# Projecting the first queries from raw activations and correcting them for layer normalisation afterwards

## The chip, the cores and the metric

The kernel runs on one NeuronCore of a Trainium2 chip. The metric is the device time of one execution in microseconds (us); the time before is 212.38 us, the median of 3 runs.

## The reference

A transformer block of 2048 tokens and width 640, in bfloat16: the input is normalised, and a local dilated attention and a dense GELU network run side by side on the normalised tokens; both results are added to the raw input.

```python
xn  = layernorm(x)                        # (x - mean) / sqrt(var + 1e-5), no affine part
qkv = xn @ wqkv                           # 640 -> 3*640; 32 heads of 20
# each token attends to itself and 7 earlier ones, 2 apart: s, s-2, ..., s-14
logits = einsum(q, k gathered) * 20**-0.5 ; attn = softmax(logits, over the 8)
A = einsum(attn, v gathered) @ wo
B = gelu(xn @ w1 + b1) @ w2 + b2          # 640 -> 1536 -> 640
return x + A + B
```

## The kernel before, in words

The tokens are split into 4 chunks of 512 (`CH`), each of 4 blocks of 128 rows. A chunk goes through these stages:

- **Statistics and normalisation.** VectorE takes mean and variance of each block (`st`, L409 and L411; the block's halves are two instructions); ScalarE takes the square root (`rs`, L430), VectorE the reciprocal (`rc`, L434). In the first chunk (n = 0) VectorE normalises (`xn`, L450), TensorE transposes 128x128 pieces (`tp`, L465), and VectorE or ScalarE copies them into `xnT` (`tc`, L470). In later chunks ScalarE normalises (L446) and a transposing DMA, issued from SyncE, writes `xnT` (L477). Block 1 of the first chunk has its sums taken on ScalarE (`sm`, `sq`, L417 and L426).
- **Projections.** In chunk 0, q of the first two blocks is made in 50 matmuls of 128 columns (`ga`, `gb`, `gd`, `ge`, L522), each as soon as a block's transposes are there; k, v and the second half of q are made in pairs of blocks, 256 columns wide (`hj`, L553). A name such as `hj011` is read which matrix (0 q, 1 k, 2 v), which pair of blocks, which group of output rows. Later chunks use 512 columns (`pj`, L509). ScalarE copies the results from PSUM (`gc`, `hc`, `pc`).
- **Attention.** VectorE multiplies q by the eight shifted k (`qk`, L583, 8 instructions per chunk), TensorE sums over each head (`lg`, L608), VectorE and ScalarE do the softmax, DMAs spread the weights over 128 partitions (`xd`, `xs`), VectorE multiplies v (`av`, L681) and adds (`ad`, `ot`).
- **Dense network.** TensorE makes the hidden layer in 12 pieces a chunk (`f1`, L703; pieces 0 to 5 use the first half of `w1_sb`, 6 to 11 the second), ScalarE applies GELU (`ge`, L714), and TensorE adds the second layer and the output projection in one accumulation (`o`, L734 and L736).

All work of PE, DVE, ACT and SP is issued in one order written out by hand, the list `ORDER`; each engine takes its own tasks from it in that order and waits where an input is late. A planner's costs (`make_plan`) stand in the file but only the list decides. POOL is scheduled by the program text. PSUM has four rotating banks for projections and hidden pieces (`psA`), two for logits (`psL`) and two for outputs (`psO`).

The inputs arrive through one queue issued from SyncE: x block 0, then `wq`, `wk`, x blocks 2 and 3, `wv`, the other x, and the two halves of `w1`; x block 1 and `b1` are issued from ScalarE. Ten matmuls on constants (`WARM`, L776) run while nothing has arrived.

```python
def load_w(s):
    nc.sync.dma_start(wqkv[s][:], wqkv_v[:, :, s * D : (s + 1) * D])
...
for name in ORDER:
    pieces[name]["fn"]()
```

Of the kernel before, what the change touches and what calls it, by code (L numbers as in the profile page):

```python
# [77 lines left out]
WARM = 10  # L78
# [6 lines left out]
pad01 pad02 st00a st00 sm rs00 me nm rc00 sq xn00a xn00b tp00a tp00b tc00a rs01 tb ga tc00b rc01 xn01 gb2 b1 tp01  # L85
gb3 tc01a tc01b gb4 gd gc0 ge st03a hj101 gc4 st03 st02a rs03 hj102 st02 hc101 hj100 rs02 hc102 rc02 rc03 gc1 hj200
xn03 xn02 hc100 st11a tp03 tp02 st13a tc03 hj201 st11 tc02 st10a hj202 hc200 st12a hj012 st10 hj010 st13 hc012 hc202
st12 hj111 hc010 hc201 hj011 rs1 hc111 rc1 st21a hj110 hc011 st22a st22 hj112 hc110 st20a hj212 st33a hc112 f102
xn10 qk031 hc212 f100 xn13 tc10 qk001 ge02 f109 qk020 hj210 pad11 tc13 ge09 hj211 qk010 xn11 f108 hc211 qk000 ge00
f101 tc11 qk011 f105 ge01 ge08 qk021 f104 xn12 f1011 tc12 ge04 qk030 f1010 ge011 st23a st21 lg00 ge010 st20 ld lg01  # L90
ge05 st23 lg02 lg03 st31a rs2 pj114 mk m0 pj102 pc114 st32a st30a pj110 pc102 mx0 hc210 pj111 pc110 st32 ex0 pj101
rc2 st31 st30 pj100 st33 pj112 ss0 pc100 pc101 pj104 xn21 ri0 pj103 tc21 pc104 at0 pc111 pj113 pc103 pc112 pj123
pc113 xn23 qk120 f113 pc123 tc23 xn22 f103 qk111 pj121 ge03 qk121 f118 xd0 qk130 ge13 f107 ge18 f112 qk100 ge07
pad21 f106 ge12 qk110 xs0 f115 ge06 qk131 xw0 f110 rs3 qk101 o020 tc22 xn20 o021 ge15 lg10 lg11 av011 lg12 pc121
tc20 lg13 ge10 rc3 pj120 av000 o022 pc120 av031 xn32 o023 pj122 tc32 av021 f111 pc122 m1 xn30 pj124 ge11 av030 tc30
pad12 pj214 av020 pj204 pc214 pj203 pc204 av001 pj211 pc203 av010 pc124 pj202 xn33 mx1 pc211 pj210 tc33 xn31 ad01
pj221 pc210 pc202 pj223 tc31 pj201 ad00 pj220 pc201 pc223 pj213 xp0 pj200 pc213 ad02 pc221 pj212 pc220 pc200 pj224
pc212 ex1 xb0 ot0 pj310 f1110 qk231 pc310 o024 qk220 pj300 oc02 ss1 pad31 od02 o000 o001 qk200 o002 o003 ri1 o004
at1 pj313 qk201 xd1 oc00 o010 pc313 qk211 pc300 pj301 xs1 qk210 o011 o012 qk221 o013 xw1 pj303 qk230 o014 xp1 xb1
lg20 oc01 lg21 av130 pc303 lg22 pc224 lg23 av100 o030 f138 av110 o031 od00 ge38 av111 pj312 o032 pc301 m2 ge110 f117  # L100
pc312 av131 f116 av120 pj304 pj302 mx2 o033 pc302 av121 ge16 f121 ge17 ad11 f1111 xp2 f1210 ge21 xb2 ge111 o034
ge210 av101 pad22 pc304 f119 ad10 pj311 pj222 pc311 xb3 oc03 pj314 ad12 ge19 od01 f114 od03 f125 ge14 pc222 ot1
pj324 pad32 pc314 ex2 o100 qk331 pj322 qk321 o101 ge25 o102 ss2 o103 pj323 ri2 o104 qk330 pc323 pc322 pj320 at2 oc10
pj321 pc320 qk311 xd2 xs2 o110 pc324 qk301 o111 pc321 o112 qk310 f120 qk300 f126 xw2 f130 ge26 qk320 f127 xl lg30
ge27 lg31 av201 lg32 lg33 o113 m3 o114 av211 f1311 oc11 av200 od11 o120 o121 od10 av221 o122 av230 o123 o124 av220
f1211 oc12 mx3 od12 o130 av210 o131 ge20 ge30 f124 ex3 ad20 f123 o132 ge311 o133 av231 o134 ge24 ss3 f128 ge211 oc13
f129 ad21 ge23 f122 ge29 ge28 f131 ge22 ri3 o210 at3 f135 ad22 o211 xd3 f134 f1310 ot2 o212 ge310 ge31 o213 xs3 o214
xw3 f137 oc21 ge34 od21 o220 av311 o221 o222 av300 o223 av310 o224 f136 av321 oc22 od22 o230 av301 o231 od13 o232
av320 o233 av331 o234 av330 f132 oc23 od23 o200 ad31 o201 ge32 ge36 o202 ge37 f139 ad30 f133 ge39 ge35 o203 ge33
o204 ad32 o310 oc20 o311 o300 ot3 o301 o302 o303 o304 o312 oc30 o313 od30 o320 od20 o321 o322 o323 o314 o324 oc31  # L110
od31 o330 oc32 o331 od32 o332 o333 o334 ohi oclo ochi
# [3 lines left out]
def make_plan(fns, offsets={}):  # L115
# [11 lines left out]
    def turned(n, pair=None):  # L127
        if n:
            return [f"tc{n}{bl}" for bl in range(BPC)]
        every = ["tc00a", "tc00b", "tc01a", "tc01b", "tc02", "tc03"]  # L130
        return every if pair is None else every[4 * pair : 4 + 4 * pair]

    def done(n, which):
        if n:
            return [f"pc{n}{which}{to}" for to in range(KT)]
        return (["gc0", "gc1", "gc4"] if which == 0 else [f"hc{which}0{g}" for g in range(len(COLS))]) + [
            f"hc{which}1{g}" for g in range(len(COLS))
        ]

    pl.add("tb", PE, 0.1, -99, ["tp00b"], f("tb"))  # L140
    pl.add("b1", VE, 0.1, -90, ["tb"], f("b1"))
    for n in range(NCH):
        base = n * PERIOD
        prev = base - PERIOD
        early = base + (-37.0 if n == 1 else -85.0)
        xnT, q, k, v, oT = (("xnT", n), ("q", n), ("k", n), ("v", n), ("oT", n))
        hTs = [("hT", n, ft) for ft in range(FT)]

        for bl in range(BPC):
            land = (3.2, 3.65, 9.3, 9.3)[bl] if n == 0 else (0.0, 13.3, 17.6, 17.6)[n]  # L150
            r = -40 if n else -90
            if n == 0 and bl == 1:
                pl.add("sm", SE, 0.84, -99, [], f("sum1"), after=land)
                pl.add("nm", SE, 0.22, -99, ["sm"], f("neg1"))
                pl.add("me", VE, 0.12, -98, ["sm"], f("mean1"))
                pl.add("sq", SE, 0.93, -99, ["nm"], f("sq1"))
                pl.add("rs01", SE, 0.3, -99, ["sq"], f("sqrt", 0, 1, 2), table="sqrt")
                pl.add("rc01", VE, 0.16, -99, ["rs01", "me"], f("rstd", 0, 1, 2))
                continue
            pl.add(f"st{n}{bl}a", VE, 0.42, r, [], f("st", n, bl, 0), [("stats", n, bl)], land)  # L160
# [4 lines left out]
        if n > 0:  # L165
            pl.add(f"rs{n}", SE, 0.3, -98, [f"st{n}{bl}" for bl in range(BPC)], f("sqrt", n, 0, BPC), table="sqrt")
            pl.add(f"rc{n}", VE, 0.25, early + -4.0, [f"rs{n}"], f("rstd", n, 0, BPC))
        for bl in range(BPC):
            xn, tp = ("xn", n, bl), ("acc", "tp", n, bl)
            if n > 0:  # L170
                pl.add(f"xn{n}{bl}", SE, 0.81, early + -4.0, [f"rc{n}"], f("xn", n, bl), [xn])
                pl.add(f"tc{n}{bl}", DQ, 3.0 if n > 1 else 2.7, early - 3.0, [f"xn{n}{bl}"], f("td", n, bl), [xn, xnT], 23.0)
                continue

            if bl == 0:
                for u, a, b, eng, own in (("a", 0, 2, VE, "lo"), ("b", 2, KT, SE, "hi")):
                    us = (b - a) / KT
                    pl.add(f"xn00{u}", VE, 0.06 + 0.5 * us, -99, ["rc00"], f("xn", 0, 0, a, b), [xn])
                    pl.add(f"tp00{u}", PE, 0.54 * us, -99, [f"xn00{u}"], f("tp", 0, 0, a, b, own), [xn])
                    pl.add(f"tc00{u}", eng, 0.16 + 0.49 * us, -99, [f"tp00{u}"], f("tc", 0, 0, a, b, eng), [xnT])  # L180
                continue
            pl.add(f"xn0{bl}", VE, 0.42, -99, [f"rc0{bl}"], f("xn", 0, bl), [xn])
            pl.add(f"tp0{bl}", PE, 0.3, -99, [f"xn0{bl}"], f("tp", 0, bl, 0, KT), [xn, tp])
            for u, a, b, eng in (("a", 0, 2, VE), ("b", 2, KT, SE)) if bl == 1 else (("", 0, KT, SE),):
                pl.add(f"tc0{bl}{u}", eng, 0.16 + 0.49 * (b - a) / KT, -100 if bl == 1 else -99, [f"tp0{bl}"], f("tc", 0, bl, a, b, eng), [tp, xnT])
# [10 lines left out]
        if n == 0:  # L196
            wq, wk, wv = 6.1, 8.5, 11.6
            A, B, C = ("acc", "qa"), ("acc", "qb"), ("acc", "qc")
            pl.add("ga", PE, 0.056 * 10, -60, ["tc00a"], f("ga", 0, 2), [xnT, A, B], wq)
            pl.add("gb2", PE, 0.056 * 5, -60, ["tc00b", "ga"], f("ga", 2, 3), [xnT, A, B], wq)  # L200
            pl.add("gb3", PE, 0.056 * 5, -60, ["gb2"], f("ga", 3, 4), [xnT, A, B], wq)
            pl.add("gb4", PE, 0.056 * 5, -60, ["gb3"], f("ga", 4, KT), [xnT, A, B], wq)
            pl.add("gd", PE, 0.056 * 10, -59, ["tc01a", "gb4"], f("gd", 0, 2), [xnT, B, C], wq)
            pl.add("ge", PE, 0.056 * 15, -59, ["tc01b", "gd"], f("gd", 2, KT), [xnT, B, C], wq)
            pl.add("gc0", SE, 0.54, -50, ["gb4"], f("gc", 0), [A, q])
            pl.add("gc1", SE, 0.54, -50, ["ge"], f("gc", 1), [C, q])
            pl.add("gc4", SE, 0.3, -50, ["ge"], f("gc", 4), [B, q])
            for which, buf, land in ((0, q, wq), (1, k, wk), (2, v, wv)):
                for pair in range(0 if which else 1, 2):
                    for g, (a, b) in enumerate(COLS):  # L210
                        ps = ("acc", "gp", which, pair, g)
                        nm = pl.add(f"hj{which}{pair}{g}", PE, 0.55 * (b - a), -50 + which // 2, turned(0, pair), f("gp", which, pair, a, b), [xnT, ps], land)
                        pl.add(f"hc{which}{pair}{g}", SE, 0.3 * (b - a), -50, [nm], f("gq", which, pair, a, b), [ps, buf])
        for which, buf in enumerate((q, k, v)):
            for to in range(KT if n else 0):
                ps = ("acc", "p", n, which, to)
                r = early + (0 if which < 2 else 20.0)
                pl.add(f"pj{n}{which}{to}", PE, 1.08, r, turned(n), f("pj", n, which, to), [xnT, ps])
                pl.add(f"pc{n}{which}{to}", SE, 0.52, early + 0.0, [f"pj{n}{which}{to}"], f("pc", n, which, to), [ps, buf])
            if which:  # L220
                need = done(n - 1, which) if n else []
                bufs = [buf] + ([("k" if which == 1 else "v", n - 1)] if n else [])
                pl.add(f"pad{n}{which}", SE, 0.26, early if n else -50, need, f("pad", n, which), bufs)
# [64 lines left out]
def kernel(  # L288
# [37 lines left out]
    outp = ctx.enter_context(tc.tile_pool(name="outp", bufs=2))  # L326

# [7 lines left out]
    nc.gpsimd.memset(b1_rt[:], 0.0)  # L335
# [8 lines left out]
    def load_w(s):  # L344
        nc.sync.dma_start(wqkv[s][:], wqkv_v[:, :, s * D : (s + 1) * D])  # L345
# [465 lines left out]
```

## Time and profile before

| | |
|---|---|
| time, median of 3 runs (lowest, highest) | 212.38 us (212.26, 212.46) |
| profiled execution: its own time | 212.62 us |
| its span (first to last instruction) | 210.6 us |
| PE (matmul) busy | 205.5 us, 98% |
| DVE busy | 173.4 us, 82% |
| ACT busy | 111.7 us, 53% |
| POOL busy | 19.8 us, 9% |
| moved by DMA | 23.93 MB, mean 114 GB/s |

The profile is of one execution, which took 212.62 us; 2.0 us of that lie outside the span of its instructions. PE is TensorE's matmul queue, PEld its weight loads, DVE is VectorE, ACT ScalarE, POOL GpSimd, SP SyncE (SPq and POOLq are the DMA-issuing sides of their queues). "x" before a number counts instructions. In a timeline a row is a start, a duration, and the merged instructions; square brackets give the idle time before them and what ended it. A matmul's listed duration includes its passage through the array, so a row of them is shorter than the sum of its parts.

### The profile page before, as it was taken

Reading aid. Unit: us, or ns where it says so; the run is one execution under the profiler, and the core shown is the slowest. Engines: PE = TensorE matmul, PEld = TensorE weight load, DVE = VectorE, ACT = ScalarE, POOL = GpSimd, SP = SyncE. Lnnn points to the kernel's source line nnn. Section 1 sums busy time; section 2 is a strip of 40 time slices with the busy share of each in tenths; the row PEclk is TensorE's granted clock in tenths of the full one; section 3 lists DMA queues with packets and bytes.
Section 4 is the critical chain, followed back from the end, with each engine's and each line's share of the span. In section 5 each row is a group of like instructions: output and inputs, shape, how many; then the busy total and the mean of one; then the engine's idle time right before and its main releaser. Section 6 shows DMA issues by size and latency. Waiting matters only on the chain.

```text
span 210.6 us, 3645 instructions
## 1 busy us (share of the span) xinstructions
PE 205.5 (98%) x1511; PEld 118.5 (56%) x1535; DVE 173.4 (82%) x178; ACT 111.7 (53%) x193; POOL 19.8 (9%) x37
## 2 busy tenths in 40 slices
PE   8999999999999999999999999999999999999994
PEld 2999656554465555555654555565554455555552
DVE  3587998969979999997899999989999829997001
ACT  5576977889786748330727487321396221441120
POOL 2000000000000002110400600101101011101130
PEclk9999999999999999999999999999999999999999
DMA  6999416924932173569296690621122571212224
GB/s 221 364 363 372 90 33 188 382 56 82 142 72 42 20 187 34 93 94 224 79 150 218 93 156 3 139 93 13 24 29 34 100 127 21 24 27 31 31 21 75
DMA packets 24072, 23.93 MB, mean 114 GB/s; under 512 B 9080, under 2 KB 21880, under 8 KB 24056
## 3 DMA queue, kind: packets, MB, share of 16 engines
q1 hardware_dynamic: 17008, 14.68, 25.1%
q0 software_dynamic: 4144, 4.92, 17.5%
q10 hardware_dynamic: 2904, 4.10, 7.0%
q8 instruction: 12, 0.20, 0.4%
q14 instruction: 4, 0.03, 0.1%
HBM read 10.00 MB, written 7.54 MB: 83 GB/s over the span
## 4 chain that ended last, share of the span: by engine, by line
PE 87%; DMA 7%; SPq 4%; issue 1%; DVE 0%
PE lo L734 27%; PE hps L703 24%; PE pps L509 23%; PE hi L736 8%; DMA w_sb<-in_B_w_dram 7%; PE L L608 4%; SPq L342 2%; SPq L359 2%; PE gps L553 1%; SPq L345 1%; DVE osb L764 0%
## 5 line engine op out<-in xcount | busy, mean ns | idle before, releaser
L703 PE MATMUL hps<-xnT,w_sb 128*128 128x512 bf16 x235 | 55.3, 379 | 0.3
L681 DVE TENSOR_TENSOR pv<-vT,ax 128x2560 bf16<-128x2560 bf16 x32 | 45.8, 1483 | 9.1 <-DMA ax<-attn 4.6
L734 PE MATMUL lo<-w_sb,hT 128*128 128x512 bf16 x184 | 52.9, 379 | 0.1
L583 DVE TENSOR_TENSOR prod<-qT,kT 128x2560 bf16<-128x2560 bf16 x32 | 45.5, 1483 | 1.9 <-ACT kT L568 1.5
L714 ACT ACTIVATE hT<-hps,b1T 128x512 bf16<-128x512 f32 x48 | 31.6, 689 | 18.4 <-PE hps L703 16.9
L736 PE MATMUL hi<-w_sb,hT 128*128 128x128 bf16 x192 | 40.3, 219 | 0.5 <-issue 0.2
L703 PEld LDWEIGHTS <-w_sb 128*128 128x128 bf16 x240 | 22.8, 98 | 26.3 <-DMA w_sb<-in_B_w_dram 0.6
L690 DVE TENSOR_TENSOR pv<-pv 128x5120 bf16<-128x5120 bf16 x12 | 33.7, 2821 | 0.2
L741 ACT CAST osb<-lo 128x512 bf16<-128x512 f32 x15 | 8.8, 587 | 44.7 <-issue 26.7
L734 PEld LDWEIGHTS <-hT 128*128 128x128 bf16 x192 | 18.7, 98 | 22.5 <-issue 0.4
L734 PE MATMUL lo<-wo,oT 128*128 128x512 bf16 x74 | 21.9, 379 | 0.0
L747 POOL DMA_DIRECT2D out_dram<-osb x15 | 13.6, 904 | 86.2 <-ACT osb L742 80.1
L736 PEld LDWEIGHTS <-hT 128*128 128x128 bf16 x192 | 18.4, 98 | 2.7
L509 PE MATMUL pps<-xnT,wk_sb 128*128 128x512 bf16 x73 | 18.2, 379 | 0.1
L509 PE MATMUL pps<-xnT,wv_sb 128*128 128x512 bf16 x72 | 18.0, 379 | 0.1
L509 PE MATMUL pps<-xnT,wq_sb 128*128 128x512 bf16 x75 | 18.0, 379 | 0.1
L736 PE MATMUL hi<-wo,oT 128*128 128x128 bf16 x80 | 16.9, 219 | 0.3
L409 DVE BATCH_NORM_STATS2 stats<-x_sb 128x6 f32<-128x320 bf16 x30 | 13.0, 467 | 4.2 <-DMA x_sb<-in_A_x_dram 4.2
L490 POOL DMA_DIRECT2D out_dram<-b2bc x4 | 5.3, 1465 | 98.6 <-DMA out_dram<-x_sb 98.6
L568 ACT CAST qT<-pps 128x512 bf16<-128x512 f32 x15 | 8.7, 590 | 8.8 <-PE pps L509 8.8
L734 PEld LDWEIGHTS <-oT 128*128 128x128 bf16 x80 | 7.8, 98 | 9.4
L509 PEld LDWEIGHTS <-wk_sb 128*128 128x128 bf16 x75 | 8.6, 118 | 7.3 <-issue 0.2
(75 smaller groups left out, 198.7 us busy)
## 6 DMA issues: line engine op xcount, KB each, us to landing
w_sb<-in_B_w_dram SPq DMA_DIRECT2D x4, 960.0 KB, 11.4
out_dram<-osb POOLq DMA_DIRECT2D x15, 160.0 KB, 3.4
ax<-attn SPq DMA_DIRECT2D x8, 256.0 KB, 4.7
ax<-attn ACTq DMA_DIRECT2D x8, 256.0 KB, 4.3
out_dram<-b2bc POOLq DMA_DIRECT2D x3, 640.0 KB, 6.6
x_sb<-in_A_x_dram SPq DMA_DIRECT2D x1, 1280.0 KB, 14.0
out_dram<-x_sb ACTq DMA_DIRECT2D x1, 1120.0 KB, 4.6
wq_sb<-in_A_wqkv_dram SPq DMA_DIRECT2D x1, 800.0 KB, 4.8
```

The source lines that it names most:

```text
L409: nc.vector.bn_stats(stats[:, i, :], x_sb[:, b, i * (D // 2) : (i + 1) * (D // 2)])
L509: nc.tensor.matmul(ps[:], lhsT=wqkv_p[which][:, ti, to, :], rhs=xnT[:, ti, :], start=(ti == 0), stop=(ti == KT - 1),)
L568: nc.scalar.copy(dest[:, to, off : off + CH], tiles["pps", n, which, to][:])
L583: nc.vector.tensor_tensor(out=prod[:, i, :, :], in0=qkv_tile(n, 0)[:], in1=qkv_tile(n, 1)[:, :, off : off + CH], op=ALU.mult,)
L681: nc.vector.tensor_tensor(out=pv[:, i, :, :].rearrange("p t (j c) -> p t j c", j=BPC), in0=qkv_tile(n, 2)[:, :, off : off + CH].rearrange( ...
L690: nc.vector.tensor_tensor(out=ta[:], in0=ta[:], in1=tb[:], op=ALU.add)
L703: nc.tensor.matmul(ps[:], lhsT=w1_sb[:, ti, ft * P : (ft + 1) * P], rhs=tiles["xnT", n][:, ti, :], start=(ti == 0), stop=(ti == KT - 1),)
L714: nc.scalar.activation(hT[:], tiles["hps", n, ft][:], ACT.Gelu_apprx_tanh, bias=b1T[:, ft : ft + 1], scale=1.0)
L734: nc.tensor.matmul(lo[:], lhsT=lhs, rhs=rhs[:, 0:CH], start=first, stop=last)
L736: nc.tensor.matmul(hi[:, 0 : D - CH], lhsT=lhs, rhs=rhs[:, CH:D], start=first, stop=last)
L741: nc.scalar.copy(osb[:, 0:CH], tiles["lo", n, bl][:])
L747: nc.gpsimd.dma_start(rows, tiles["osb", n, bl][:], accum_op=ALU.add)
```

## The change

- **q of blocks 0 and 1 from raw x.** TensorE transposes the raw blocks (`tr`, 10 transposes), VectorE copies them to a tile `xr` (`ra`, `rb`, in two cuts per block) beside columns of ones, and 30 matmuls (`qr0`, `qr1`, `qr2`; 20 of 258 columns and 10 of 130) give the raw projection together with the column sums of `wq`, in the logits' and outputs' PSUM banks. Layer normalisation is affine per token, so q = (raw - mean x column sum) / deviation: the means and reciprocal deviations (`rn`) are written to DRAM (`rw`) and read back spread over 128 partitions (`rr`), both by POOL's DMA queue; VectorE subtracts (`qc0`, `qc1`) and GpSimd multiplies (`qd0`, `qd1`). The 50 matmuls L522 and the copies `gc0`, `gc1`, `gc4` go. Normalisation and transposes of the blocks stay, since k, v and the dense network use them; block 0 is no longer cut in two.
- **wq and wv arrive in two loads each**, cut after row tile 2 of 5; v of the first pair begins with the first part (`hv0`, `hv1`, loops turned so that the row tile is outermost).
- **Statistics of the last chunk on ScalarE**: sums (`su`), negated means (`nq`) and squares (`sv`), and `mq` on VectorE, in place of eight `st` instructions and four aggregations.
- **Smaller ones**: 6 warm-up matmuls, not 10; `b1` loaded by POOL's queue and its transpose `tb` placed after the first k piece; `w2` in one load; `ORDER` written anew throughout, with the same tasks otherwise.

The core of the diff (the new order is cut to its beginning):

```diff
-WARM = 10
+WARM = 6
...
-pad01 pad02 st00a st00 sm rs00 me nm rc00 sq xn00a xn00b tp00a tp00b tc00a rs01 tb ga tc00b rc01 xn01 gb2 b1 tp01
-gb3 tc01a tc01b gb4 gd gc0 ge st03a hj101 gc4 st03 st02a rs03 hj102 st02 hc101 hj100 rs02 hc102 rc02 rc03 gc1 hj200
-xn03 xn02 hc100 st11a tp03 tp02 st13a tc03 hj201 st11 tc02 st10a hj202 hc200 st12a hj012 st10 hj010 st13 hc012 hc202
-st12 hj111 hc010 hc201 hj011 rs1 hc111 rc1 st21a hj110 hc011 st22a st22 hj112 hc110 st20a hj212 st33a hc112 f102
-xn10 qk031 hc212 f100 xn13 tc10 qk001 ge02 f109 qk020 hj210 pad11 tc13 ge09 hj211 qk010 xn11 f108 hc211 qk000 ge00
+st00a tr0 st00 sm tr1 ra0 rs00 ra1 nm rb1 sq qr0 rc00 xn00 rb0 rs01 pad01 me tp00 rc01 pad02 xn01 qr1 tc00 rn tp01
+rw qr2 tc01a tc01b hj101 st02a tb st02 hj100 rr st03a rs02 hc101 b1 hj102 rc02 xn02 hc100 st03 tp02 hj202 hc102 rs03
+hv0 tc02 rc03 xn03 st13a tp03 hv1 st11a tc03 st11 hc202 qc0 hj110 hc201 hj012 st13 hc110 qd0 hj010 st10a hc200 st12a
+hc012 qc1 hj112 hc010 hj111 hc112 st10 qd1 hj011 st12 hc111 st23a rs1 hj212 rc1 hc011 hj211 xn10 qk030 xn11 f102
+qk031 hc211 tc10 hj210 hc212 ge02 qk020 f109 f105 qk021 ge09 tc11 hc210 f1010 pad11 qk000 ge05 f104 xn12 qk010 ge010
...
-    def load_w(s):
-        nc.sync.dma_start(wqkv[s][:], wqkv_v[:, :, s * D : (s + 1) * D])
+    def load_w(s, *cuts):
+        for a, b in zip((0, *cuts), (*cuts, KT)):
+            nc.sync.dma_start(wqkv[s][:, a:b, :], wqkv_v[:, a:b, s * D : (s + 1) * D])
...
-    nc.scalar.dma_start(b1_rt[0:FT, :], B_b1.rearrange("(t p) -> t p", p=P))
-    load_w(0)
+    load_w(0, 2)
     load_w(1)
     load_x(2, BPC)
-    load_w(2)
+    load_w(2, 2)
...
+    nc.gpsimd.dma_start(b1_rt[0:FT, :], B_b1.rearrange("(t p) -> t p", p=P))
...
+    def do_su(bl):
+        nc.scalar.activation(sink[:], x_sb[:, LAST + bl, :], ACT.Identity, accum_out=acc3[:, bl : bl + 1])
+    def do_sv(bl):
+        b = LAST + bl
+        nc.scalar.activation(
+            sink[:], x_sb[:, b, :], ACT.Square, bias=neg3[:, bl : bl + 1], scale=RD, accum_out=mv[:, b, 1:2]
+        )
...
+    def do_qr(a, b):
+        qL, qlo, qhi = q_raw()
         for ti in range(a, b):
+            first, last = ti == 0, ti == KT - 1
+            for to, ps in enumerate((qL[:, 0, 0:WIDE], qL[:, 1, 0:WIDE], qlo[:, 0:WIDE], qhi[:, 0:WIDE])):
+                nc.tensor.matmul(
+                    ps,
+                    lhsT=wqkv_p[0][:, ti, to, :],
+                    rhs=xr[:, ti, ONE : BOTH + 2],
+                    start=first,
+                    stop=last and to > 1,
+                    skip_group_check=True,
+                )
...
+    def do_rw():
+        nc.gpsimd.dma_start(rn_d[:], rn[:])
+    def do_rr():
+        tiles["rnbc"] = axp.tile([P, 4, CH], F32, tag="ax", name="rnbc")
+        flat = rn_d[:].rearrange("p v b -> (p v b)")
+        nc.gpsimd.dma_start(tiles["rnbc"][:, 0, :], flat.unsqueeze(0).to_broadcast([P, 4 * P]))
...
+        for to, c, src in parts[3 * g : 3 + 3 * g]:
+            nc.vector.scalar_tensor_tensor(
+                out=qraw[:, to, :].rearrange(fold, b=2),
+                in0=rows_of(1),
+                scalar=colsum[:, c : c + 1],
+                in1=src,
+                op0=ALU.mult,
+                op1=ALU.add,
+            )
...
+            nc.gpsimd.tensor_tensor(
+                out=dst, in0=src, in1=rows_of(0).unsqueeze(1).to_broadcast([P, n, 2, P]), op=ALU.mult
+            )
```

## The prediction

> **What bounds the kernel now.** I read the page's busy table first, then the chain of work that ended last in order of time, then the timelines of PE, DVE and ACT over the first 24 us, since every edit but one lies there.
>
> ```profile
> PE 205.5 (98%) x1511; PEld 118.5 (56%) x1535; DVE 173.4 (82%) x178; ACT 111.7 (53%) x193; POOL 19.8 (9%) x37
> ```
>
> TensorE is busy nearly throughout. Something can be gained only where it idles or does no useful work. The end of the chain, by its times:
>
> ```profile
> 9.74 13.95 DMA w_sb<-in_B_w_dram
> 23.73 1.25 PE hps L703 x5
> ...
> 30.68 2.97 PE hps L703 x13
> 33.65 2.30 PE L L608 x80
> ```
>
> The chain leaves PE at 23.73: the second half of w1 landed just then, and PE had waited 0.6 us for it (the one DMA in PEld's list of waits). Before that the end was set by the DMA queue. The logits (L608) start at 33.65 and the last matmul ends at 207.88 (a row at 207.44 lasting 0.44). I count PE's work between them at its issue spacings, from the timelines: 0.216 us for 512 columns (5 in 1.08), 0.109 for 256 (the v matmuls: 10 from 12.06 to 13.15), 0.056 for 128, 0.575 for a group of 20 logits. It gives 173.9 us against 174.2 elapsed: hardly 0.3 us is idle after 33.65. The start:
>
> ```profile
> 0.78 4.42 PE L776 MATMUL idle<-const-bfloat16-1.0 128*128 128x512 bf16 x10 [0.78 <-PEq L795]
> 5.39 0.79 PE L465 MATMUL tp<-ident,xn 128*128 128x128 bf16 x5 [0.19 <-DVE xn L450]
> ...
> 7.38 2.12 PE L522 MATMUL gps<-xnT,wq_sb 128*128 128x128 bf16 x35
> 9.33 2.89 PE L553 MATMUL gps<-xnT,wk_sb 128*128 128x256 bf16 x25
> ```
>
> Useful work begins at 5.39, behind the statistics; k begins at 9.33, although wk is issued at 1.67 and lands 6.7 us later, near 8.35. About 1 us can be won there, if what follows can use it.
>
> **What the Trainium skill says.** "TensorE: Matmul & The Clock Gate", Part 1: TensorE starts at half clock and is released after a busy window of about 3.4 us; the windows run free. Part 4 says that transposes do not count as busy in the same way. The trace agrees on the half rate: ten warm-up matmuls of 512 columns take 4.42 us, 0.43 apart, against 0.216 later; after 6.23 all run full. It does not show how much activity is enough. "DMA: Bandwidth & Descriptors", anatomy of a DMA: a POOL-issued DMA costs about 2 us plus its bytes at 436 GB/s, and all queues share the same 16 engines. Here 160 KB from POOL lands in 3.4 us, compatible, and the engines are full from 3 to 21 us (363 to 372 GB/s in the slices). "GPSIMD Engine Reference", section 3.1: two-input arithmetic takes about 2.6 cycles per element at 1.2 GHz; no such instruction is in this trace.
>
> **The change part by part.**
>
> *q from raw x.* x block 0 lands at 3.24 (its statistics start then), block 1 at 3.62. Ten transposes at half clock take 1.1 us and finish near 4.5. DVE ends block 0's statistics at 4.37, then copies `ra0`, `ra1` at 0.29 each (L470's 128x256 row): 4.95. The first 320 KB of wq should land near 4.8 (800 KB landed at 6.0 with the same stream). So `qr0` starts near 5.05. On DVE follow `rb1` 0.40 (between 0.29 for 256 columns and 0.48 for 384 on ACT), `rc00` 0.16, `xn00` 0.45, `rb0` 0.40, `me` and `rc01` 0.3, `xn01` 0.45, to 7.1. PE: `qr0` is 8 x 0.110 + 4 x 0.057 = 1.11, to 6.15; five transposes 0.29; `qr1` 0.55 to 7.0; transposes at 7.2 to 7.5; `qr2` 1.11 to 8.6. ACT's copy `tc01b` is done by 8.2, wk by 8.35. k starts at **8.6 instead of 9.33**. All q matmuls cost 2.77, the removed 50 x 0.056 = 2.8; the ten extra transposes (0.56 warm) fall into time when PE waited. Four fewer warm-ups only make room, if the clock is there.
>
> *Up to the second half of w1.* The new order puts more ahead of its first use, `f109`: all 125 projection matmuls of 256 columns (13.65), ten transposes (0.58), `tb` (0.1) and `f102` (1.08) = 15.4 us after k starts, so PE is there at 24.0. Before, 14.2 us lay between (105 matmuls, the transposes, `f102`, `f100`), so it was there at 23.5, delayed to 23.73. But the DMA stream now carries `rr`: 2 KB to each of 128 partitions is 256 KB, 0.7 us at 364 GB/s, ahead of w1's end. `rw` is 2 KB in 16-byte pieces, 0.05 to 0.3. I take w1 at 24.4 (bounds: 23.7 if hidden, 24.8). Two more loads on SP cost 0.4 to 0.5 us each in issue (L345's rows) and move the later ones back; w1 lands 14 to 15 us after its issue, so its queue covers that. `f109` runs at 24.4. From there to the logits lie 8.64 us: eight f1 pieces at 1.08, against 9.74 before. Adding the 0.1 by which that stretch exceeded its sum, the logits start at **33.15 instead of 33.65**.
>
> *Does DVE deliver by then?* In this row the eight products take 11.3 us:
>
> ```profile
> 21.48 11.30 DVE L583 TENSOR_TENSOR prod<-qT,kT 128x2560 bf16<-128x2560 bf16 x8 [0.44 <-ACT kT L563]
> ```
>
> They need q. `rn` (two small instructions) ends at 7.4; POOL's issue (0.9, L747) and the fixed 2 us put `rw` at 10.3; `rr` takes 3.5 by that price, 4.7 by the nearest row (ax, 256 KB): 13.8 to 15.0. DVE reaches `qc0` at about 15.2: three half statistics and an aggregation of x blocks 4 to 7 (1.5 us) stand before it, which began at 13.34 before and may begin 0.3 later. `qc0` is 0.16 + 3 x 0.425 (the f32 128x256 row, L645), `qc1` 0.32 + 2 x 0.425. With 1.5 us of statistics between, `qc1` ends at 19.3. GpSimd's `qd1`, 512 elements, takes 1.1 by the skill's price, so q is complete at 20.5. If GpSimd takes twice that it is 21.6. What queues behind `qc0` on DVE is the statistics of chunk 1 and then the products; 19.3 and two block ends (0.65 each), a half (0.44) and `rc1` (0.34) give a start near 21.4 and an end at 32.7, **0.4 us ahead of PE**. Taking ACT's `gc` copies away (1.55 us) hides behind PE either way.
>
> *Last chunk's statistics.* DVE loses 8 x 0.467 + 4 x 0.209 = 4.6 us. ACT gains 4 x 0.85 + 0.2 + 4 x 0.95 = 7.4 us (durations of L417 and L426 with the accumulator read), and I place them at 30 to 34 and 46 to 62. In these windows (columns PE, PEld, DVE, ACT) ACT has 3.8 and 3.7 us left of each 20:
>
> ```profile
> 27.00:47.00 20.00, 19.89 (x161) 10.99 (x162) 17.85 (x33) 16.17 (x25) 0.00 (x0) 1.00 0.56 173
> 47.00:67.00 20.00, 19.84 (x169) 10.73 (x171) 18.22 (x15) 16.34 (x24) 0.00 (x0) 1.00 0.49 86
> ```
>
> The `hc` copies move earlier and make some room, and four PSUM banks let ACT trail by three pieces (3.2 us). I take 0, with 0 to 1 us as bounds. Table loads stay 13. DVE's gain is not on the path.
>
> *The rest*, at 0: v stands 3.7 us of PE's work behind the start of k, at 12.3, and wv landed at 11.5, so its two loads gain nothing, and lose nothing unless `rr` pushes them by 0.8. `b1` is first used by GELU at 24.6, w2 at 57; both loads have tens of us, or at least 15, of cover. If w2's one load came late, outputs would wait; it has over 20 us.
>
> **Sum.** From the logits to the end PE has the same 173.9 us, so the start's 0.5 us is the whole: own time 212.62 - 0.5 = 212.1. The profiled execution lies 0.24 above the median, so **211.9** against 212.38. About 0.2% (0.42 us) is what a measurement of this kernel tells from no change.
>
> **The rivals.**
>
> 1. *The clock gate comes late (slower).* Warm-up now ends near 3.35; then come transposes, and a pause until 5.05. The switch lies between 5.2 and 6.23 in the trace of before, at the end of a window filled mostly by warm-up matmuls. In the same window now, two fifths are matmuls and a third transposes. If that is too little, the next chance is 3.4 us later, near 9.5. At half clock `qr0` to `qr2` with the transposes, 3.35 us of work, would have done 2.2 by then; k starts at 10.6, `f109` at 26.0, the logits at 34.75: 1.1 us slower, 213.5. It decides against the change once k starts after about 9.4. For it: the thinner activity; against it: if transposes count, the window is as full.
> 2. *The gain is hidden by w1 (no change).* If the two POOL DMAs or their small descriptors delay w1 to 24.9, the logits start at 33.65 and the time is 212.4. For it: the full DMA engines; against it: only 256 KB.
> 3. *ACT becomes the bound (slower).* If it cannot absorb 7.4 us in 27 to 67, PE waits for banks by up to 1 us: 212.9. For it: 81% busy; against it: short queues.
> 4. *q late through GpSimd or the round trip.* Once the products start more than 0.4 us after 21.4 it passes one for one to the logits; 1 us gives 212.5. The same in kind as 3.
>
> **How the numbers follow.** The main case has chance 0.58 with its own range 211.5 to 212.2 (w1 at 23.7 to 24.7), of which 0.47 is beyond 0.2%; rival 2 0.14, mostly within 0.2%; rival 1 0.18; rivals 3 and 4 together 0.10. So faster 0.49, same 0.20, slower 0.31. The range 211.3 to 213.4 leaves out the cases with all gains at once and the worst of rival 1.
>
> **What would show it.** k (256-column matmuls on wk) from 8.6, `qr` rows spaced 0.11 and not 0.215, PEld's wait for w1 near 24.4, logits near 33.15, no new PE wait on ACT between 33 and 67. Wrong: `qr` at half rate, the first q products waiting for POOL, or a PSUM wait after the logits.

## The result, and the profile after

The changed kernel takes **218.97 us** (median of 4 runs, 217.72 to 219.87) against 212.33 for the kernel before on the same chip: ratio 1.031, interval 1.025 to 1.037. It is 6.6 us slower; 211.9 was forecast. Its profiled execution took 219.72, with a span of 217.9 instead of 210.6.

The busy table and the clock row of the page after:

```profile
PE 209.1 (96%) x1521; PEld 119.2 (55%) x1521; DVE 173.3 (80%) x179; ACT 116.8 (54%) x207; POOL 25.5 (12%) x45
...
PEclk9999958999999999999999999999999999999999
```

The clock row of the page before:

```profile
PEclk9999999999999999999999999999999999999999
```

TensorE's busy time grew by 3.6 us although it has hardly more work to do: the clock row falls to 5 and 8 tenths in the sixth and seventh slice, between 27 and 38 us, so the same matmuls lasted longer there. The rest of the 7.3 us is idle time. The chain of work that ended last, in order of time (start, duration, what), tells where:

```profile
7.34 5.64 DMA rn_d<-rn
12.98 0.29 issue
13.27 6.68 DMA rnbc<-rn_d
...
20.06 1.90 DVE qraw L642 x3
...
23.47 1.23 DVE qraw L642 x2
...
26.18 0.56 ACT qT L688
...
28.96 11.55 PE hps L828 x40
40.52 2.30 PE L L733 x80
```

Before, the chain ran from w1's load to PE and the logits started at 33.65. Now it runs through both legs of the round trip, then VectorE's corrections, then ScalarE, and the logits start at 40.52, 6.9 us later. From there to the end of the span lie 177.4 us instead of 177.0. So nearly the whole loss was made before the logits, and 0.4 us after them.

VectorE's wait for the rows and its products, from its timeline:

```profile
20.06 1.90 DVE L642 SCALAR_TENSOR_TENSOR qraw<-rnbc,colsum,qL 128x256 f32<-128x256 f32 x3 [3.76 <-DMA rnbc<-rn_d]
...
26.84 11.31 DVE L708 TENSOR_TENSOR prod<-qT,kT 128x2560 bf16<-128x2560 bf16 x8 [0.17 <-ACT qT L688]
```

PE's waits (total, times, longest), its timeline after the longest of them, and the stretch of f1, `hps`, that the low clock falls on (columns PE, PEld, DVE, ACT, POOL, PEclk, DMA share, GB/s):

```profile
PE gps L678 <- ACT qT L688: 2.3, 1, 2.3
...
PE hps L828 <- ACT vT L688: 0.8, 1, 0.8
PE gps L678 <- DMA wk_sb<-in_A_wqkv_dram: 0.7, 1, 0.7
```

```profile
26.79 1.41 PE L678 MATMUL gps<-xnT,wv_sb 128*128 128x256 bf16 x10 [2.27 <-ACT qT L688]
```

```profile
29.00:40.40 11.40, 11.40 (x40) 4.43 (x39) 11.33 (x14) 9.52 (x17) 0.00 (x0) 0.76 0.32 61
```

At 24.5 PE has no free PSUM bank, since ScalarE does not empty them. It stands for 2.3 us, until 26.8, and from 28.2 on for another 0.8 us. In between, the clock falls to half, and stays there for 6.8 us (27.76 to 34.58 in the clock record). Forty f1 matmuls take 11.4 us instead of the 8.6 that 40 x 0.216 make, and PE reaches the logits after VectorE's last product (38.15) instead of just before it. Why ScalarE stood still is in its timeline:

```profile
20.76 0.58 ACT L688 CAST kT<-gps 128x512 bf16<-128x512 f32 x1 [0.72 <-PE gps L678]
25.97 0.30 ACT L471 ACTIVATE std<-mv,eps_t 128x4 f32<-128x4 f32 x1 [4.63 <-DVE mv L437]
```

The square root of chunk 1 (`rs1`) waits 4.63 us for statistics that VectorE computes only after its late corrections, and the copy of a finished PSUM bank (`hc011`) stands behind it.

### The profile page after: what moved, and what is told of

Same layout as the page of the kernel before. It is cut to its first block, busy times and chain, and to the rows that moved or that the text cites. A ratio compares the mean times of both kernels' runs of the same rounds, so it can differ in the third digit from the quotient of the medians.

```text
span 217.9 us, 3664 instructions
## 1 busy us (share of the span) xinstructions
PE 209.1 (96%) x1521; PEld 119.2 (55%) x1521; DVE 173.3 (80%) x179; ACT 116.8 (54%) x207; POOL 25.5 (12%) x45
## 4 chain that ended last, share of the span: by engine, by line
PE 85%; DMA 7%; DVE 3%; ACT 2%; issue 1%; DVEq 0%
PE lo L859 27%; PE hps L828 25%; PE pps L549 22%; PE hi L861 7%; PE L L733 4%; DMA rnbc<-rn_d 3%; DMA rn_d<-rn 3%; DVE qraw L642 1%; DMA x_sb<-in_A_x_dram 1%; DVE stats L435 1%; ACT xn L487 1%; ACT xn L452 0%; ACT xn L443 0%; DVE mv L437 0%; ACT std L471 0%
## 5 line engine op out<-in xcount | busy, mean ns | idle before, releaser
L828 PE MATMUL hps<-xnT,w_sb 128*128 128x512 bf16 x240 | 59.0, 393 | 0.8 <-ACT vT L688 0.8
L859 PE MATMUL lo<-w_sb,hT 128*128 128x512 bf16 x192 | 54.5, 379 | 0.0
L828 PEld LDWEIGHTS <-w_sb 128*128 128x128 bf16 x240 | 23.4, 101 | 29.0 <-issue 5.1
L872 POOL DMA_DIRECT2D out_dram<-osb x15 | 13.0, 867 | 106.8 <-ACT osb L867 95.1
L859 PE MATMUL lo<-wo,oT 128*128 128x512 bf16 x80 | 23.1, 379 | 0.0
L435 DVE BATCH_NORM_STATS2 stats<-x_sb 128x6 f32<-128x320 bf16 x22 | 9.7, 471 | 5.0 <-DMA x_sb<-in_A_x_dram 5.0
L693 ACT CAST kT<-pps 128x512 bf16<-128x512 f32 x15 | 8.6, 587 | 9.2 <-PE pps L549 9.1
```

The source lines that it names most:

```text
L435: nc.vector.bn_stats(stats[:, i, :], x_sb[:, b, i * (D // 2) : (i + 1) * (D // 2)])
L828: nc.tensor.matmul(ps[:], lhsT=w1_sb[:, ti, ft * P : (ft + 1) * P], rhs=tiles["xnT", n][:, ti, :], start=(ti == 0), stop=(ti == KT - 1),)
L859: nc.tensor.matmul(lo[:], lhsT=lhs, rhs=rhs[:, 0:CH], start=first, stop=last)
L872: nc.gpsimd.dma_start(rows, tiles["osb", n, bl][:], accum_op=ALU.add)
```

## The experiments

The working theory: the round trip, 12.6 us long instead of the 6.4 to 7.6 of the prediction, starts all of this. The rivals were the split loads (k late), the statistics on ScalarE, and the correction itself.

### The round trip

**rows_const**: the changed kernel with constant rows in place of mean and deviation.

```diff
-        nc.gpsimd.dma_start(rn_d[:], rn[:])
+        pass
...
-        nc.gpsimd.dma_start(tiles["rnbc"][:, 0, :], flat.unsqueeze(0).to_broadcast([P, 4 * P]))
+        nc.gpsimd.memset(tiles["rnbc"][:, 0, :], 1.0)
```

> The changed kernel, with the two POOL DMAs of the round trip left out and the 512 row values set to 1.0 by a GpSimd memset, so the correction of q uses no real means and deviations. Theory T (q is late because of the round trip, everything else follows from it): VectorE's wait of 3.8 us before its first correction is gone, corrections start near 16.3, the first q product near 23 and not 26.8, the logits near 34.5 and not 40.5, TensorE has no idle time over 1 us, its clock stays full, and the time is 212.5 to 214. Rival R (the f32 corrections, GpSimd's multiplies and ScalarE's extra 7.4 us keep q late in any case): products start after 25 and the time stays above 216.

Measured: 213.80 (ratio 1.0064, 1.005 to 1.0078). Its chain has no round trip, and PE's longest wait for an input is 1.2 us, for the second part of wq:

```profile
23.92 11.32 DVE prod L708 x8
...
35.28 2.37 PE L L733 x80
```

So the round trip and what it sets off cost 5.2 us of the 6.6, both in the medians (218.97 - 213.80) and at the logits (40.52 - 35.28). About 1.4 us has other causes.

**act_queue**: the changed kernel with both DMAs of the round trip issued by ScalarE (`nc.scalar.dma_start` in both lines).

> The changed kernel, with both DMAs of the round trip issued from ScalarE's queue in place of POOL's. Theory B (the DMA engines are full of the loads until 21 us, and any small DMA waits behind what they hold): the two still take about 5 and 6 us, and the time stays at 217 to 220. Theory P (it is POOL's own path that is slow): about 2.5 and 3 us, the rows land near 13, and the time is as without the round trip, 212.5 to 214.5.

Measured: 217.12 (1.022, 1.014 to 1.031). The tile view of `rn_d` gives the time to landing of both legs:

```profile
L610 ACTq DMA_DIRECT2D rn_d<-rn x1: 335/335/335, 7.4 to 7.4; - x1
...
DMA to landing us min/median/max: 5.8/5.9/6.1
```

The legs are as long as from GpSimd (5.64 and 6.68 there), so the issuing engine is not the cause. ScalarE itself now stands 4.1 us in front of the second issue.

**quiet_probe** and **busy_probe**: the kernel before with the same pair of transfers, which nothing waits for, once near 25 us and once near 6 us (from chunk 0's statistics; the edit of the second, the first differs in source and place).

```diff
+        if n == 0 and b0 == 1:
+            nc.gpsimd.dma_start(pb_d[:], mv[:, 0:2, :])
+            pb = axp.tile([P, 4 * P], F32, tag="ax", name="pb")
+            nc.gpsimd.dma_start(pb[:], pb_d[:].rearrange("p v b -> (p v b)").unsqueeze(0).to_broadcast([P, 4 * P]))
```

> The kernel before, with a round trip of the same shape (16 bytes of each of 128 partitions to DRAM, then 2 KB to each of 128 partitions) issued from POOL after the first GELU, near 25 us, when the loads are in and the DMA engines mostly idle; nobody uses the result. Theory B (full engines): each of the two DMAs lands within 2 to 3.5 us. Theory P (POOL's path): 5 to 6.7 us each, as in the changed kernel. The time stays within 0.3 us of 212.3 in both, as nothing waits for it.

> The kernel before with the round trip added at its place in the changed kernel (mean and variance of blocks 0 and 1, 2 KB out and 256 KB back on GpSimd's queue from about 6 us on), for which nothing waits; loads unsplit, b1 on ScalarE's queue as before. Theory F (full engines make each leg long): legs of 5.0 to 7.0 us, against 3.3 and 3.5 of the same pair at 25 us; time 212.4 to 213.1, the 256 KB being 0.7 us of DMA ahead of w1. Rival (something else in the changed kernel stretched them): legs of 3 to 4.5 us.

The tile view of `pb_d` (both legs) in quiet_probe, then in busy_probe:

```profile
L720 POOL DMA_DIRECT2D pb_d<-hT x1: 712/712/712, 25.6 to 25.6; - x1
...
DMA to landing us min/median/max: 3.0/3.3/3.5
```

```profile
L442 POOL DMA_DIRECT2D pb_d<-mv x1: 822/822/822, 6.0 to 6.0; - x1
...
DMA to landing us min/median/max: 5.9/6.3/6.7
```

The same 2 KB out and 256 KB back take 3.0 and 3.5 us at 25 us, and 5.9 and 6.7 us from 6 us on, where the DMA row is full, in a kernel that has nothing else of the change. **This settles the length of the legs**: it comes with the moment, not with the issuing queue or the rest of the change. That it is the full engines which make the moment slow is read from the DMA row, not tested apart. The record of packets tells where the time goes: from the issue to the first packet 4.4 and 4.1 us pass in busy_probe (4.0 and 4.2 in the changed kernel), against 1.3 and 1.4 in quiet_probe, so most of the extra time lies ahead of the data. Times: 212.55 (1.0011, 0.9994 to 1.0028) and 213.39 (1.0035, 0.9997 to 1.0072); the traffic alone costs at most 1.5 us by the interval, perhaps nothing.

**after_unsplit**: the changed kernel with wq and wv in one load each (`load_w(0)`, `load_w(2)`).

> The changed kernel with wq and wv each in one load again; all else stays, the round trip through DRAM too. Theory L (the split makes one DMA engine fall 2 us behind, and both legs of the round trip wait for that engine's packets, so it lengthens them): wk lands near 8.4, rw's leg takes 3.5 to 4.5 instead of 5.64 and rr's 4.5 to 5.5 instead of 6.68, corrections start at 16.5 to 18, time 214.5 to 216.5. Theory F (the legs are long because the engines are full, split or not): legs still 5 to 7 us, corrections at 19 to 20, time 217 to 219; only k starts earlier.

Measured: 218.21 (1.027, 1.024 to 1.030). The legs are still 5.75 and 6.50 us in its chain, and the corrections start at 19.81. Theory L, that the split lengthens them, falls.

**rs1_later**: the changed kernel with `rs1` and `rc1` moved in `ORDER` behind three copies.

```diff
-... hc111 st23a rs1 hj212 rc1 hc011 hj211 xn10 qk030 xn11 f102 qk031 hc211 tc10 hj210 hc212 ge02 ...
+... hc111 st23a hj212 hc011 hj211 hc212 hc211 rs1 rc1 xn10 qk030 xn11 f102 qk031 tc10 hj210 ge02 ...
```

> The changed kernel with ScalarE's square root of chunk 1 (rs1) and what hangs on it moved behind the copies hc011, hc212 and hc211. Theory C (the square root, waiting for statistics that stand behind the late corrections, blocks the copies; TensorE then idles some 2.3 us for PSUM banks and its clock drops to half for 6.8 us): now no such wait, f1 at full clock, the products start at 25.9 to 26.3 and end near 37.4, the logits start there instead of at 40.5, time 215.7 to 216.7, and TensorE idles about 3 us ahead of the logits instead. Rival: the clock drops for another reason, or drops after that idle stretch all the same: 218 to 219.5.

Measured: 217.94 (1.024, 1.019 to 1.029); the profiled run 217.52, its clock full. PE no longer waits for `qT`, the logits start at 38.26 (40.52 in the changed kernel), and the times of the two profiled runs differ by 2.2 us. But the products start at 27.00, not near 26.0: the rows land 0.3 us later in this profile (the corrections start at 20.37 instead of 20.06), and from there VectorE works without a gap; in the changed kernel it had lost only 0.17 us before the products, so there was little to gain on this side. And PE stands 2.2 us for `hT` instead, without a fall of the clock in this run:

```profile
30.82 6.64 PE L828 MATMUL hps<-xnT,w_sb 128*128 128x512 bf16 x30 [2.23 <-ACT hT L839]
```

The other three runs have mean clocks near 0.992. So the link from ScalarE's blocked queue to PE's wait is shown. That a wait of this length brings the half clock is not: it followed in one profile and not in the other (the last section has a reading of why), and the medians, 1.0 us apart, have overlapping intervals.

### The split loads

**split_wq**: the kernel before with `load_w(0, 2)` alone.

> The kernel before with one edit: wq in two loads (first two row blocks, then the other three). Tells why wk landed at 9.76 in the changed kernel and at 8.34 before. Theory S (the extra load in front of wk lets one DMA engine fall behind, so wk's last piece comes late): wk lands at 9.6 to 10.4, k starts 0.4 to 1.1 us later than 9.33; of that 0.56 us vanishes in the wait for w1's second half if that stays at 23.7, so 212.4 to 212.9. Theory N (the split costs nothing, the lateness came from b1 on GpSimd's queue or from both together): wk near 8.4 to 8.7, k at 9.33, 212.3.

Measured: 213.82 (1.0061, 1.0037 to 1.0085), so **1.3 us slower from one load cut in two**, more than the 0.6 us that was expected at most. The tile view of wk, in the kernel before and in this one:

```profile
L345 SPq DMA_DIRECT2D wk_sb<-in_A_wqkv_dram x1: 518/518/518, 1.7 to 1.7; - x1
...
DMA to landing us min/median/max: 6.7/6.7/6.7
```

```profile
L346 SPq DMA_DIRECT2D wk_sb<-in_A_wqkv_dram x1: 488/488/488, 2.2 to 2.2; - x1
...
DMA to landing us min/median/max: 8.1/8.1/8.1
```

wk is issued 0.5 us later and lands 1.9 us later. Each load's completion arrives in 16 parts. For wk they lie between 7.84 and 8.34 before; after the split between 7.95 and 10.28, fifteen by 9.11, and the loads after it have the same straggler. By the record of packets the stream as a whole runs 0.5 to 0.7 us later; the rest is the one part that is behind. Which engine lags, and why, the trace does not say. The kernel before has such a straggler too, but only in its last loads (w1's second half: fifteen parts by 22.00, the last at 23.69); the cut goes with one from the start. In the profiled run PE waited not for wk but for the second part of wq itself, whose last completion part came at 8.05, where the whole of wq had landed at 6.0 before:

```profile
8.09 0.73 PE L523 MATMUL gps<-xnT,wq_sb 128*128 128x128 bf16 x5 [1.15 <-DMA wq_sb<-in_A_wqkv_dram]
```

This run (215.62) is above all but two of the 22, and its clock fell to half from 7.95 to 11.36, so its start of k, 12.33, is not typical.

**rows_unsplit**: rows_const with wq and wv unsplit.

> The changed kernel with constant rows in place of mean and deviation (no round trip) and with wq and wv each in one load. Against the same with split loads (213.8): if the split's 1.3 us, which it cost alone in the kernel before, adds up: 212.4 to 212.8, wk near 8.4 and k at 8.7 to 9.3. Rival: the products of VectorE (23.9 there) remain the bound, whatever k does: 213.4 to 213.8.

Measured: 214.48 (1.0062, 1.0037 to 1.0086). By the median the gain of 1.3 us did not come. The runs fall into two groups, eight of 20 between 212.8 and 213.1, the other twelve above 214.3. The profiled one is of the latter, and its chain shows why:

```profile
1.20 4.72 DMA wq_sb<-in_A_wqkv_dram
5.97 0.62 PE qL L587 x2
6.59 0.22 PE qlo L587
...
10.26 0.11 PE qlo L587
...
11.15 1.09 PE gps L678 x10
```

q's first matmuls wait for wq until 5.97 and then run 0.22 apart instead of 0.11: full speed came at 9.45 by the clock record, and k started at 11.15. The eight are probably those in which it came in time; none of them has a profile. This is the prediction's rival 1, in a kernel in which the wait for wq is longer than in the changed one.

**b1_pool**: the kernel before with b1 loaded on GpSimd's queue, as in the change.

> The kernel before, with one part of the change alone: b1 is loaded by POOL's queue in place of ScalarE's. In the changed kernel wk landed 1.4 us later than before (9.76 against 8.34). If POOL's descriptors disturb the stream, wk lands near 9.7 here too, k starts near 9.8, w1's second half lands later than 23.7, and the time is 0.3 to 1 us longer. If the split of wq does it, wk lands at 8.35 and the time stays within 0.2 us of 212.3.

Measured: 216.41 (1.017, 1.012 to 1.023). It tells nothing on the changed kernel's b1, since here the transpose `tb` stands early in PE's order. wk landed at 8.67, so GpSimd's queue does not make it late. What it shows is the price of an early wait of PE, by its timeline:

```profile
8.12 0.17 PE L592 MATMUL tb<-ident,b_rt 16*128 16x16 bf16 x1 [2.13 <-DMA b_rt<-in_B_b_dram]
8.22 1.79 PE L522 MATMUL gps<-xnT,wq_sb 128*128 128x128 bf16 x15
```

Fifteen matmuls that took 1.03 us before take 1.79 after a wait of 2.13 us, and k starts at 14.05 instead of 9.33.

### The other parts

**rows_contig**: rows_const with the rows contiguous.

```diff
-        return tiles["rnbc"][:, 0, :].rearrange("q (p v b) -> q v b p", v=2, b=2)[:, v, :, :]
+        return tiles["rnbc"][:, 0, :].rearrange("q (v b p) -> q v b p", v=2, b=2)[:, v, :, :]
```

> The changed kernel with constant rows, read as contiguous rows of 128 elements instead of with a stride of 4 elements (16 bytes); loads split. Theory: the stride makes the correction slow; its instruction takes 0.40 to 0.45 us instead of 0.68, GpSimd's multiply 1.0 to 1.2 instead of 1.5, the products start 1.2 to 1.4 us earlier (22.6), time 212.9 to 213.3 against 213.8. Rival: the PSUM operand in f32 sets the pace; 0.65 to 0.68, 213.8.

The tile view of `rnbc` (min/median/max ns), in the changed kernel and here:

```profile
L642 DVE SCALAR_TENSOR_TENSOR qraw<-rnbc,colsum,qL x3: 693/695/698, 20.1 to 21.3; 128x256 f32<-128x256 f32 x3
L654 POOL TENSOR_TENSOR qT<-qraw,rnbc x3: 869/1516/1555, 21.4 to 24.8; 128x512 bf16<-128x512 f32 x2, 128x256 bf16<-128x256 f32 x1
```

```profile
L642 DVE SCALAR_TENSOR_TENSOR qraw<-rnbc,colsum,qL x3: 473/473/480, 16.4 to 17.2; 128x256 f32<-128x256 f32 x3
L654 POOL TENSOR_TENSOR qT<-qraw,rnbc x3: 720/1272/1276, 17.4 to 20.1; 128x512 bf16<-128x512 f32 x2, 128x256 bf16<-128x256 f32 x1
```

The stride of 16 bytes makes the correction half as long again. Products start at 22.51, the logits at 34.22, and the time is 213.36 (1.0023, 0.9998 to 1.0047): 0.4 us less than with strided rows by the medians, 1.1 by the profiled spans. Not all of the 1.4 us by which the products start earlier comes from the rows: in the profile of rows_const the x blocks whose statistics stand ahead of the corrections landed at 15.4, here at 14.7. Now PE is the last, not VectorE: it reaches the logits 0.57 us later than before, having started k at 9.77 instead of 9.33.

**stats_act**: the kernel before with the last chunk's statistics on ScalarE (`su`, `nq`, `mq`, `sv` of the change in place of `st3x`, at about the changed kernel's places in `ORDER`).

> The kernel before with the last chunk's statistics alone moved from VectorE to ScalarE (7.4 us more on ScalarE, placed as in the changed kernel). Theory of the prediction: 0, so 212.3, no new wait of TensorE on ScalarE of over 0.3 us between 30 and 67 us. Rival 3 of the prediction: up to 1 us, 212.9 to 213.3, with TensorE waiting for PSUM banks or for hT in that stretch.

Measured: 213.07 (1.0026, 1.0005 to 1.0048), 0.6 us slower. The chain between 44 and 60 us:

```profile
45.42 0.49 ACT kT L594
45.91 0.82 ACT sink L450 x2
...
47.20 0.98 ACT kT L594 x2
...
48.21 11.32 DVE prod L609 x8
...
59.57 0.50 PE L L634 x9
```

One statistic (`sink`) lies ahead of the copies of q and k that chunk 1's products need. They start at 48.21 instead of 47.52, and chunk 1's logits at 59.57 instead of 59.22. This is the loss after the first logits: 0.3 to 0.5 us in the profiles with this part at its place, and 0.9 in act_queue.

**f109_later**: the kernel before with the first use of w1's second half 1.1 us of PE's work later (`f109` behind `hj210` in `ORDER`).

> The kernel before with f109, the first user of w1's second half, moved behind hj210 (1.1 us of TensorE's work later). If the wait of 0.56 us for w1 was the only obstacle ahead of the logits: logits at 33.1 to 33.2 instead of 33.65, 211.8 to 211.9. Rival: the products of VectorE (which ended at 32.8) or ScalarE's copies take over: 212.1 to 212.4.

Measured: 212.46 against 212.44 (0.9989, 0.996 to 1.0018). The wait for w1 is gone, and the logits start at 33.47, 0.18 us earlier than in the profile of before, with k 0.18 us later in this run. A gain of 0.4 us at this place is at the edge of what can be measured, and was not seen.

**pe_rows** and **pe_rows2**: the idea without what had cost. TensorE makes the rows; loads unsplit, rows contiguous, last statistics on VectorE. In pe_rows six warm-up matmuls and `rs1` late; in pe_rows2 ten, and `rs1` at its place.

```diff
+            nc.vector.tensor_scalar(out=diag[:, b, :], in0=ident[:], scalar1=rstd[:, b : b + 1], scalar2=None, op0=ALU.mult)
+            nc.vector.tensor_scalar(out=diag[:, 2 + b, :], in0=ident[:], scalar1=mv[:, b, 0:1], scalar2=-1.0, op0=ALU.mult, op1=ALU.mult)
...
+        nc.tensor.matmul(tiles["rows"][:], lhsT=ones[:, 0:P], rhs=diag[:].rearrange("p v n -> p (v n)"), start=True, stop=True)
...
+        nc.scalar.copy(tiles["rnbc"][:, 0, :], tiles["rows"][:])
```

> The idea of the change without what the earlier runs showed to cost: rows of mean and deviation made by TensorE (ones times a diagonal, one matmul of 512 columns, copied to SBUF by ScalarE) instead of the round trip, contiguous rows, wq and wv in one load each, the last chunk's statistics on VectorE, the square root of chunk 1 behind the copies. If nothing else is hidden: rows ready near 9.5, corrections no longer waiting for them, products at 21.5 to 22.5, logits at 33.2 to 33.9, time 211.9 to 212.6. Rival: VectorE's 2 to 3 us of corrections stay on the path to the products: logits at 34.5 to 35, 213.2 to 213.8.

> pe_rows with its two own faults mended: ten warm-up matmuls instead of six, and the square root of chunk 1 back at its place ahead of the copies. Rows from TensorE, contiguous, loads unsplit, last statistics on VectorE. If those two faults were all: q's first matmul at 6.0 at full clock, k near 9.4 (no earlier than before, since wq lands at 5.9), products at 22.0 to 22.6, logits at 33.5 to 34.0, 212.3 to 212.9: equal to before at best. Rival: something else of the change costs over 1 us: 213.4 to 215.

pe_rows: 217.35 (1.022, 1.020 to 1.024). The clock opened at 9.24, k started at 11.32, and `rc1`, behind the late `rs1`, held the products until 25.98. pe_rows2: 214.57 (1.0080, 1.0057 to 1.0103), 213.93 in the profiled run. There q started at 5.96 at full clock, k at 9.54, the products at 22.14 and the logits at 33.79, all as expected and level with before. But 178.3 us follow instead of 177.0, with a wait of 1.0 us for products. Its statistics of chunk 3 stand elsewhere in the order than before, so this last loss belongs to my order, probably, and was not taken further. No version was faster than the kernel before.

### The account

In the profiled spans the 7.3 us lost divide so: round trip and its consequences 5.24 (logits of after less rows_const), strided rows 1.06 (rows_const less rows_contig), the late k 0.57 (rows_contig less before), the statistics on ScalarE 0.43 (logits to end). The last three make 1.4 us in the median of rows_const, so these single profiles put the rows' share too high: had x landed as late as in rows_const, the products of rows_contig would have started 0.7 us later and its logits about 0.4, an estimate from the two chains. Of the 5.24, some 2.3 are the half clock and the rest is VectorE's lateness: its products ended at 38.15, and at full clock the logits would have started just behind them, as in rs1_later at 38.26, not at 40.52.

## Why the prediction was wrong

**The step that failed is the price of the two DMAs.** `rw` was put at 10.3 (issue 0.9 and a fixed 2 us) and `rr` at 13.8 to 15.0; they landed at 12.98 and 19.95. The working used the fixed cost from the Trainium skill, "DMA: Bandwidth & Descriptors", anatomy of one DMA, and checked it on a 160 KB row of 3.4 us. That row is of output stores, the first of them at 88 us, when the loads were long in. The same text noted that the engines are full from 3 to 21 us, and used that for bandwidth alone. The same page, "Latency and other measured facts", says that memory latency rises from 0.2 to 2 us at high load and calls it the main part of the fixed cost. The two probes agree in direction, and with 2.9 and 3.2 us more they go further; but most of their extra time lies ahead of the first packet, so no run shows that memory latency is the reason. Even the prediction's upper end, the ax row of 4.7 us, was too short.

**Rival 4 was the right mechanism and mis-sized.** It said that lateness passes to the logits one for one, allowed 1 us, shared a chance of 0.10, and had no branch in which the slack of 0.4 us was gone many times over. VectorE stood 3.76 us for the rows. Without the round trip the products would still have started at 23.92, not 21.4: VectorE was ready for `qc0` at 16.3, not 15.2, because x blocks 4 to 7 landed later than before, and its corrections and GpSimd's multiplies were longer than said.

**What queues behind was followed on VectorE only.** The statistics behind `qc0` were named, but not `rs1`, which waits for them on ScalarE, nor `hc011` behind it. From there came PE's 2.3 us and, by the reading in the last section, the stretch at half clock.

**Sizes of single terms.** The correction: 0.425 taken from a contiguous row, 0.63 measured (1.90 for three), about 1.0 us over five. The Trainium skill, "SBUF — State Buffer", under "Door 1: The DMA port swizzle", says that SBUF is read in lines of 16 bytes and that crossing to a new line costs; with a stride of 16 bytes each element is on a new line, and rows_contig shows the difference. `qd1`: 1.1 said, 1.52 measured with strided and 1.27 with contiguous rows. k: 8.6 said, 9.80 measured, because wk landed at 9.76 and not at 8.35. The two extra loads were costed as 0.4 to 0.5 us of issue, and the lagging part was not thought of; alone this cost 1.3 us. ACT's 7.4 us: 0 taken, 0 to 1 bounded, 0.6 measured. The sign of a new wait was looked for at PSUM; it was at VectorE's wait for the copies of q and k.

**What held.** q from raw x ran at full clock from 4.84, a little earlier than the 5.05 said; matmuls of 258 columns are 0.11 apart. Rival 1 fell for this kernel, though rows_unsplit and pe_rows show how near it was: it took the moment of the switch in the profile before (6.12) for that of every run, and the profiles have it anywhere from 3.64 to 9.45. In the profile of the changed kernel it came at 3.86, which by this spread was luck. Rival 2 was overtaken: w1 bound nothing. The reading that PE has hardly any idle time after the logits held to 0.4 us. The size of what could be won, 0.5 us, was also small against what could be lost. That should have widened the range upward: where q came straight from PSUM before, it now hung on two transfers in a row and on three engines.

## What to carry to other kernels

Price a DMA from a row of the same stretch of the profile: transfers of 2 and 256 KB among full engines took 5.6 to 6.7 us here, and 3.0 to 3.5 us in a quiet stretch. When an instruction becomes late, follow the queues of all engines whose order is fixed: the costly one was not the engine that waited, but the next, where a short square root stood ahead of copies that free PSUM. And a load that is cut in two is not free, even where its issue is: look at the last of its completion parts.

## What was not expected of the hardware

- One extra load at the head of the stream left one of the 16 completion parts of the next loads 1.1 to 1.2 us behind the next-to-last one (split_wq: the second part of wq 6.92 and 8.05, wk 9.11 and 10.28, wv 12.27 and 13.46). In the changed kernel the parts of wk are spread over 1.7 us (8.06 to 9.76) without a single straggler.
- The clock changes in fixed steps, and what seems to count is how much of one step PE waits. In the 15 profiles with a clock record every change lies a whole number of steps of 3.41 us after the first full speed; in the changed kernel full speed came at 3.86, and 27.76 and 34.58 follow it by 7 and 9 steps. PE's 2.27 us of waiting (24.5 to 26.8) fell inside one step, 24.35 to 27.76, and half speed followed; the same was seen with 2.2 us in a step in after_unsplit and 2.0 in b1_pool. In rs1_later a step ended at 29.29, in the middle of the wait of 2.23 us (28.6 to 30.8), which left 0.7 in one step and 1.5 in the next, and the clock stayed full. So whether a wait of this length costs the clock depends on where it falls, and the start of the steps differs from run to run. Where the limit lies is open: 1.6 us in a step were followed by half speed in split_wq, 1.7 in after_unsplit were not. No run moved the steps on purpose; this is read from the traces, not tested.
